# State-space convolution beside a feed-forward block on one core: borrowed PSUM banks and a new VectorE order at the outset, responses and another pair's first transform step in one run, the last token tile stored by halves

## The chip, the core and the metric

The kernel runs on one core of a Trainium2 chip, in one launch. The metric is the time of an execution in device microseconds. The engines are named as in the profile: PE is TensorE's matmul side and PEld its weight loads, DVE is VectorE, ACT is ScalarE, POOL is GpSimd, and SP is SyncE, which here only issues DMAs. PSUM has eight banks of 128 x 512 float32; a matmul writes into one of them, and ACT or DVE reads it out.

## The reference, cut to what matters

```python
xn = layernorm(u)                               # u: 2048 tokens x 576
h  = silu(xn @ w1)                              # w1: 576 x 4608
ffn = h @ w2                                    # w2: 4608 x 576
K[d, l] = Re(sum_n C[d,n] * dt[d]*B[d,n] * exp(dt[d]*A[d,n] * l))    # 128 states n, 2048 lags l
ssm = causal_convolution(xn, K) + xn * Dskip    # the reference does it by FFTs of length 4096
return u + ssm + ffn
```

All is float32 outside. Where the kernel multiplies in its faster float32 form it splits each operand into a high and a low part (names ending in `h` and `l`) and adds three products.

## The kernel before, in words

**Two streams.** A main stream, the generator `ffn`, does the feed-forward block. A side stream, the generator `side`, does everything else: loading and normalizing tokens, the convolution's kernel and spectra, and the stores. `weave` steps the main one and lets the side one go on at given marks. This gives the order of the program; a scheduler then plans the order of each engine's queue when the kernel is built, by a simulated timeline. `tc.high_priority()` moves instructions up in that plan, and `behind(ins)` forbids an instruction to stand ahead of `ins`. Each engine works through its queue in order, so an instruction that waits holds up all that is queued behind it.

**The feed-forward block.** 2048 tokens in two halves of two blocks of 512; 4608 hidden columns in nine chunks of four slots of 128. For a block and a chunk, `up` computes the slots (`ph`, L313 to L315: per slot 12 products of a 128-row part with `xh`/`xl` and two with the remaining 64 rows `x4`), ACT takes the SiLU out of PSUM (`gf`, L321) and casts it (`gh`, L322), DVE subtracts (`gl`, L323). `down` multiplies 128 tokens with the four slots, in two halves of 288 output columns (`po`, L338: 12 products each), and DVE adds the result to the token's sum (`acc`, L342). The weights of the next chunk come in meanwhile: `load_w1` and `load_w2` issue DMAs into `w1r` and `w2r` (L291), ACT casts them to `w1h` and `w2h` (L300), DVE subtracts to `w1l` (L282) and `w2l` (L302). At the turn from the first half of the tokens to the second, `next_xt` loads the transposed tokens `xl` (L352) on POOL's queue and `split_xt` splits them.

**PSUM banks.** `ps1` has two banks for `ph`, `ps2` three for `po`, and `pss` three for all of the side stream: token transposes `pt` (L124), `kp` and `z` (below), `pu` of the spread step, and the spectral step's products. A new tile of a pool waits until the oldest of its banks has been read out.

**The outset.** PE first runs filler matmuls on zeros (`idle`). `phase0` loads token tiles 0 to 7 by pairs into `acc`, on SP's queue alone or on SP's and ACT's; `norm` takes their statistics on DVE (L186), the inverse deviation `sd` on POOL, and normalizes; `put_xt` transposes on PE into `pt`, and ACT and DVE split that into `xh`, `xl`, `x4`. The later tiles 8 to 15 (`xj`) go through the same `norm` a little later, by `late`. The first chunk's slots are computed in two stretches of 256 columns, `up(blocks[0], t, 0, 256)` and then `(256, 512)`, because only the first tokens are there. `pins` holds the instructions behind which others are put: tiles 2 and 3 behind the first `w1l`, tiles 4 to 7 behind the last transposes' split of tile 3 (`xt3`), the four `w2l` behind the last `w1l`.

**Responses and transforms.** `kgen` computes the convolution's kernel for the 576 channels in 36 chunks of 16 channels. Per chunk DVE and ACT build tables `S` and `C` of sines and cosines times magnitudes (ACT: L631 and L633). Per two chunks (a pair; 18 in all) PE multiplies them into `kp` (L674, 64 products on 128x32 tiles into one bank), ACT copies it out (`kt`, L681), and PE applies the first step of a transform to `kt` (`z`, L689, eight products on 64x128 tiles into two banks); ACT copies `z` to `stage`, from which it is stored to DRAM every second pair. The kp products of a pair are held together by `behind(first)`, the z products likewise, so that each makes one run of PE's queue; po and ph of the main stream stand between the two. Each step of the side stream also takes the next step of `spread`, the tokens' own first transform: it copies and splits a tile (`sp`) and multiplies it in two halves, two products each (`pu`, L155, L156).

**The end.** The last `down` steps finish one token tile after the other; after them the tiles that are left are stored by `store`, in four quarters of 32 partitions on alternating queues (L177).

Of the kernel before, what the change touches and what calls it, by code (L numbers as in the profile page):

```python
# [11 lines left out]
F32 = mybir.dt.float32  # L12
# [3 lines left out]
ALU = mybir.AluOpType  # L16
# [3 lines left out]
P = 128  # L20
L = 2048
D = 576
NS = 128
FF = 4608
NJ = 16
NKT = 4
HD = D // 2
# [16 lines left out]
def kernel(  # L44
# [21 lines left out]
    nc = tc.nc  # L66
# [45 lines left out]
    acc = {}  # L112
# [23 lines left out]
    def behind(ins):  # L136
        return tc.issue_after(ins) if ins is not None else nullcontext()
# [36 lines left out]
    def store(t, j, engines):  # L174

        for ps, v, eng in quarters(ov, engines):
            eng.dma_start(v[:, j:j + 2] if len(t.shape) > 2 else v[:, j], t[ps])  # L177

    def norm(p0, js, xs):

        n = len(js)
        st = p0.tile([P, 2, 2, 6], F32, tag="st", name="st")
        mv = p0.tile([P, 2, 2], F32, tag="mv", name="mv")
        for i in range(n):
            for h in range(2):
                nc.vector.bn_stats(out=st[:, i, h, :], in_=xs[i][:, h * HD:(h + 1) * HD])  # L186
            nc.vector.bn_aggr(out=mv[:, i, :], in_=st[:, i, :, :])
        sd = p0.tile([P, 2], F32, tag="sd", name="sd")
        mb = p0.tile([P, 2], F32, tag="mb", name="mb")
        nc.vector.tensor_scalar(sd[:, :n], mv[:, :n, 1], 1e-5, None, op0=ALU.add)  # L190
        pins["sd"] = nc.gpsimd.tensor_tensor(sd[:, :n], sd[:, :n], mhalf[:, :n], op=ALU.pow).ins
        xn = p0.tile([P, 2, D], F32, tag="xn", name="xn") if js[0] < 8 else pairs[js[0]]
        for i, j in enumerate(js):
            if j % 2 == 0 or j < 2:
                pins["xn"] = nc.vector.tensor_scalar(xn[:, i, :], xs[i], mv[:, i, 0:1], sd[:, i:i + 1],
                                                 op0=ALU.subtract, op1=ALU.mult).ins
            else:
                nc.vector.scalar_tensor_tensor(mb[:, i:i + 1], mv[:, i, 0:1], -1.0, sd[:, i:i + 1],
                                               op0=ALU.mult, op1=ALU.mult)
                nc.scalar.activation(xn[:, i, :], xs[i], AF.Identity,  # L200
                                     scale=sd[:, i:i + 1], bias=mb[:, i:i + 1])
        return xn

    def phase0(p0, js, idle=None):

        xs = load_x(js[0], accp, "acc", (nc.sync, nc.scalar) if js[0] < 4 else (nc.sync,))
        acc.update(zip(js, xs))
        yield
        if js[0]:
            with behind(pins["w1l0"] if js[0] == 2 else None):  # L210
                normed(p0, js, xs)
        else:
            for j, xj in zip(js, xs):
                with behind(pins["xn"] if j else None):
                    normed(p0, (j,), (xj,))
                if not j:
                    pins["xt0s"] = pins["xt_s"]
                with behind(pins["pt"]):
                    idle(3 if j else 9)
        pins[f"xt{js[1]}h"] = pins["xt_h"]  # L220
        pins[f"xt{js[1]}"], pins[f"xt{js[1]}s"] = pins["xt_v"], pins["xt_s"]
        yield
# [23 lines left out]
    def ffn():  # L246
# [6 lines left out]
        def load_w1(half, c, t):  # L253

            f = c * FT + t
            first = half == 0 and c == 0
            last = half == 1 and c == NCH - 1
            r1 = (pa if first and t else yp if last and t else wp).tile([P, 5, 2 * P], F32, tag="w1r", name="w1r", bufs=1)
            fs = slice(f * P, (f + 2) * P)
            v1 = w1[0:512, fs].rearrange("(k p) f -> p k f", p=P)  # L260
            eng = nc.sync
            if first and t == 0:
                eng = nc.gpsimd
                nc.sync.dma_start(r1[:, 0:2, :], v1[:, 0:2])
                nc.scalar.dma_start(r1[:, 2:4, :], v1[:, 2:4])
            else:
                eng.dma_start(r1[:, 0:4, :], v1)
            eng.dma_start(r1[0:64, 4, :], w1[512:576, fs])
            pins["load"] = eng.dma_start(r1[64:128, 4, :], w1[512:576, fs]).ins
            R1[half, c, t] = r1  # L270

        def split_w1(half, c, t):
            first = half == 0 and c == 0
            r1 = R1.pop((half, c, t))
            for i in range(2):
                h1 = wp.tile([P, 5, P], F32R, tag="w1h", name="w1h", bufs=FT + 1)
                l1 = wp.tile([P, 5, P], F32R, tag="w1l", name="w1l", bufs=FT + 1)
                src = r1[:, :, i * P:(i + 1) * P]
                with behind(pins.get("gh", pins["xt1s" if t + i else "xt0s"])):
                    nc.scalar.copy(h1, src)  # L280
                with behind(pins["xn" if t else "xt1"] if first else None):
                    pins["w1l"] = nc.vector.tensor_sub(l1, src, h1).ins  # L282
                pins.setdefault("w1l0", pins["w1l"])
                W1[half, c, t + i] = h1, l1

        def load_w2(half, c, t):
# [7 lines left out]
        def split_w2(half, c, t):  # L294
            first = half == 0 and c == 0
            r2 = R2.pop((half, c, t))
            h2 = wp.tile([P, D], F32R, tag="w2h", name="w2h", bufs=FT + 1)
            l2 = wp.tile([P, D], F32R, tag="w2l", name="w2l", bufs=FT + 1)
            with behind(pins["xt_s"] if first else pins["gh"]):
                pins["w2h"] = nc.scalar.copy(h2, r2).ins  # L300
            with behind(pins["w1l"] if first else None):
                nc.vector.tensor_sub(l2, r2, h2)  # L302
            W2[half, c, t] = h2, l2

        def up(blk, t, a=0, e=512):
# [1 line left out]
            half, c, b = blk  # L307
            xh, xl, x4 = xts[2 * half + b]
            h1, l1 = W1[half, c, t]
            ph = ps1.tile([P, 512], F32, tag="ps1", name="ph")[:, a:e]  # L310
            for n, (w, v) in enumerate(((h1, xh), (h1, xl), (l1, xh))):
                for kt in range(NKT):
                    nc.tensor.matmul(ph, w[:, kt, :], v[:, kt, a:e], start=n + kt == 0, stop=False)  # L313
# [248 lines left out]
    def kgen():  # L562
        fT, phiT = kf["f"], kf["phi"]
        with tc.tile_pool(name="kg", bufs=1) as kg:
# [53 lines left out]
                return th  # L618

            stage = None  # L620
            tabs = []
            nxt = head(0)
            al = powers(0)
            for i in range(NCK):
# [52 lines left out]
                                if begins:  # L677
                                    first = mm.ins
                tabs = []
                kt = kg.tile([P, 512], F32, tag="kt", name="kt")  # L680
                nc.scalar.copy(kt, kp)  # L681

                z = [pss.tile([P, 512], F32, tag="pss", name="z") for _ in range(2)]
                first = None
                for eg in range(4):
                    for h in (1, 0):
                        rows = slice(64 * h, 64 * h + 64)
                        with tc.high_priority(), behind(first):
                            mm = nc.tensor.matmul(z[h][:, eg * P:(eg + 1) * P], kt[rows, eg * P:(eg + 1) * P], f1[rows],  # L689
                                                  start=True, stop=True, tile_position=(64 * h, 0))  # L690
                        first = first or mm.ins
                r = (i - 1) % NRUN
                if r == 0:
                    stage = kg.tile([P, 64, NRUN * CH], F32, tag="stage", name="stage")
                sv = stage[:, :, r * CH:(r + 2) * CH].rearrange("p k (e h c) -> p h e k c", h=2, c=2)
                for h in range(2):
                    nc.scalar.copy(sv[:, h], z[h].rearrange("p (e k c) -> p e k c", e=4, c=2))
                if r == NRUN - 2:
                    d0 = (i // NRUN) * NRUN * CH
                    kv = d1k.rearrange("(k n) (g d) -> g n k d", n=64, g=2)  # L700
                    for gp_ in range(2):
                        nc.sync.dma_start(kv[gp_, :, :, d0:d0 + NRUN * CH], stage[gp_ * 64:(gp_ + 1) * 64])
                yield (i + 1) / NCK

        nc.gpsimd.dma_start(d1k.rearrange("(k n) d -> n k d", n=P)[0],
# [135 lines left out]
    def side():  # L841
# [3 lines left out]
        with tc.tile_pool(name="kf", bufs=1) as kfp:  # L845
            for n in ("f", "phi"):
                kf[n] = kfp.tile([P, D], F32, name=n + "T")
            with tc.tile_pool(name="par", bufs=1) as par:
                with tc.tile_pool(name="pa", bufs=4) as pa:
# [17 lines left out]
                    next(p23)  # L867
                    yield 0
                    for js in ((4, 5), (6, 7)):
                        with behind(pins["xt3"]):  # L870
                            for _ in phase0(pa, js):
                                pass
                    kf["dt"] = steps()
# [127 lines left out]
```

## Time and profile before

| | |
|---|---|
| median of 3 runs | 1114.06 us (1113.56 to 1114.08) |
| profiled execution | 1113.42 us, its span 1111.6 us |
| granted TensorE clock | 1.0 |
| PE busy | 1103.3 us, 99% of the span, 9168 matmuls |
| DVE busy | 916.9 us, 82% |
| ACT busy | 709.2 us, 64% |
| POOL busy | 69.8 us, 6% |
| DMA | 148.56 MB, 134 GB/s on average |
| chain that ended last | PE 97%: po 42%, ph 41%, kp 3%, the spectral products 6%, z 2% |

The span is the time from the first to the last recorded event of the profiled execution; the execution's own time is 1.8 us longer. Rows of the trace show a start in microseconds from the span's beginning, a duration, engine and line, what the instruction writes and reads (`out<-in`, for a matmul with its tile of rows x columns), and the repeat count of equal neighbours; in brackets how long the engine stood before it and what ended the wait. The duration of a matmul includes its way through the array, so a step of PE is read from start to start.

### The profile page before, as it was taken

What the parts mean: (1) busy time and instruction counts of PE and PEld (TensorE: products, weight loads), DVE (VectorE), ACT (ScalarE), POOL (GpSimd) and SP (SyncE); (2) the same over time, 40 slices, a digit from 0 to 9 for tenths busy, and PEclk for the clock granted to TensorE, in tenths of its full rate; (3) what the DMA queues carried; (4) which work ended last, traced back from release to release, by engine and by line L of the source; (5) the groups of instructions that cost most, each with busy time, mean ns of one, the idle gap of its engine ahead of it and who ended that gap; (6) DMA issues with size and microseconds to landing.
All of it is one profiled execution on the core that took longest, in us unless ns stands there. A gap on an engine that the chain in (4) does not pass through costs nothing.

```text
span 1111.6 us, 22913 instructions
## 1 busy us (share of the span) xinstructions
PE 1103.3 (99%) x9168; PEld 997.8 (90%) x9168; DVE 916.9 (82%) x1546; ACT 709.2 (64%) x1228; POOL 69.8 (6%) x129
## 2 busy tenths in 40 slices
PE   8999999999999999999999999999999999999998
PEld 6998999899889899899989989999999999999887
DVE  6899899999999999999999837787778778784433
ACT  5574456676777676677866536877777878773210
POOL 1100000000000000011000000000000000000111
PEclk9999999999999999999999999999999999999999
DMA  9745522425242515255844163554545445434983
GB/s 258 201 122 152 137 71 61 120 63 130 82 107 80 134 61 131 77 149 161 219 123 105 44 173 106 169 157 128 161 145 150 139 146 171 129 107 130 248 211 86
DMA packets 175563, 148.56 MB, mean 134 GB/s; under 512 B 111024, under 2 KB 142272, under 8 KB 175328
## 3 DMA queue, kind: packets, MB, share of 16 engines
q1 hardware_dynamic: 165136, 112.33, 38.7%
q0 software_dynamic: 9568, 33.62, 9.5%
q8 instruction: 72, 1.18, 0.5%
q10 hardware_dynamic: 752, 1.15, 0.4%
q14 instruction: 35, 0.29, 0.1%
HBM read 102.53 MB, written 44.61 MB: 132 GB/s over the span
## 4 chain that ended last, share of the span: by engine, by line
PE 97%; DMA 1%; DVE 0%; SPq 0%; issue 0%; ACT 0%; ACTq 0%; POOL 0%; DVEq 0%
PE po L338 42%; PE ph L313 35%; PE kp L674 3%; PE ph L314 3%; PE ph L315 3%; PE pu L804 2%; PE pb L804 2%; PE pk L804 2%; PE z L689 2%; PE pu L155 1%; DMA acc<-in_A_u_dram 1%; PE py L825 1%; PE pu L156 1%; DMA w2r<-in_B_w_dram 0%; PE pt L124 0%; DVE st L186 0%
## 5 line engine op out<-in xcount | busy, mean ns | idle before, releaser
L338 PE MATMUL po<-w2l,gh 128*128 128x288 f32 x1152 | 338.5, 295 | 0.9 <-DVE w2l L302 0.9
L338 PE MATMUL po<-w2h,gl 128*128 128x288 f32 x1152 | 336.2, 295 | 0.0
L338 PE MATMUL po<-w2h,gh 128*128 128x288 f32 x1152 | 335.8, 295 | 0.0
L338 PEld LDWEIGHTS po<-w2h,gh 128*128 128x128 f32 x1152 | 215.1, 188 | 7.6 <-issue 2.8
L338 PEld LDWEIGHTS po<-w2l,gh 128*128 128x128 f32 x1152 | 215.9, 188 | 6.1 <-DVE w2l L302 1.1
L338 PEld LDWEIGHTS po<-w2h,gl 128*128 128x128 f32 x1152 | 215.4, 188 | 0.8
L321 ACT ACTIVATE gf<-ph 128x512 f32<-128x512 f32 (+1 forms) x148 | 86.4, 585 | 142.9 <-PE ph L315 128.3
L313 PE MATMUL ph<-xh,w1h 128*128 128x512 f32 (+1 forms) x592 | 162.1, 388 | 1.2 <-ACT gf L321 1.2
L313 PE MATMUL ph<-xl,w1h 128*128 128x512 f32 (+1 forms) x592 | 161.4, 386 | 0.0
L313 PE MATMUL ph<-xh,w1l 128*128 128x512 f32 (+1 forms) x592 | 161.0, 385 | 0.0
L342 DVE TENSOR_TENSOR acc<-po,acc 128x288 f32<-128x288 f32 x288 | 126.4, 452 | 37.4 <-PE po L338 36.1
L323 DVE TENSOR_TENSOR gl<-gf,gh 128x512 fp32r<-128x512 f32 (+1 forms) x148 | 99.2, 673 | 64.8 <-ACT gh L322 64.1
L313 PEld LDWEIGHTS ph<-xh,w1l 128*128 128x128 f32 x592 | 108.1, 188 | 19.9
L313 PEld LDWEIGHTS ph<-xl,w1h 128*128 128x128 f32 x592 | 108.0, 188 | 20.0 <-DVE xl L126 0.2
L313 PEld LDWEIGHTS ph<-xh,w1h 128*128 128x128 f32 x592 | 104.5, 188 | 18.5 <-ACT gf L321 1.8
L322 ACT CAST gh<-gf 128x512 fp32r<-128x512 f32 (+1 forms) x148 | 89.8, 609 | 10.1 <-PE po L338 7.1
L631 ACT ACTIVATE c<-th,magic 128x1040 f32<-128x1040 f32 x36 | 42.1, 1169 | 37.9 <-DVE C L654 28.0
L633 ACT ACTIVATE c<-th 128x1040 f32<-128x1040 f32 x36 | 38.7, 1075 | 34.0 <-DVE th L632 34.0
L300 ACT CAST w2h<-w2r 128x576 fp32r<-128x576 f32 x72 | 46.9, 671 | 17.2 <-PE po L338 14.9
L282 DVE TENSOR_TENSOR w1l<-w1r,w1h 128x640 fp32r<-128x640 f32 x72 | 57.1, 818 | 0.2
L314 PE MATMUL ph<-x,w1h 128*128 128x512 f32 (+1 forms) x148 | 57.0, 385 | 0.0
L315 PE MATMUL ph<-x,w1l 128*128 128x512 f32 (+1 forms) x148 | 56.9, 385 | 0.0
(184 smaller groups left out, 1830.1 us busy)
## 6 DMA issues: line engine op xcount, KB each, us to landing
w2r<-in_B_w_dram SPq DMA_DIRECT2D x72, 288.0 KB, 3.7
w1r<-in_B_w_dram SPq DMA_DIRECT2D x35, 512.0 KB, 3.9
d1u<-u POOLq DMA_DIRECT2D x32, 288.0 KB, 2.6
d1k<-stage SPq DMA_DIRECT2D x18, 512.0 KB, 6.8
ur<-d1u SPq DMA_DIRECT2D x32, 288.0 KB, 3.9
kr<-d1k SPq DMA_DIRECT2D x32, 288.0 KB, 2.8
d<-yo POOLq DMA_DIRECT2D x32, 288.0 KB, 3.7
ys<-d SPq DMA_DIRECT2D x32, 288.0 KB, 11.6
```

The lines of the kernel that those rows point to most:

```text
L282: pins["w1l"] = nc.vector.tensor_sub(l1, src, h1).ins
L300: pins["w2h"] = nc.scalar.copy(h2, r2).ins
L313: nc.tensor.matmul(ph, w[:, kt, :], v[:, kt, a:e], start=n + kt == 0, stop=False)
L314: nc.tensor.matmul(ph, h1[:, 4, :], x4[:, a:e], start=False, stop=False)
L315: pins["pe"] = nc.tensor.matmul(ph, l1[:, 4, :], x4[:, a:e], start=False, stop=True).ins
L321: nc.scalar.activation(gf, ph, AF.Silu)
L322: pins["gh"] = nc.scalar.copy(gh, gf).ins
L323: pins["gl"] = nc.vector.tensor_sub(gl, gf, gh).ins
L338: pins["pe"] = nc.tensor.matmul(po[:, :HD], G[blk, t][g][:, js], W2[half, c, t][w][:, hs], start=n == 0, stop=n == 3 * FT - 1).ins
L342: nc.vector.tensor_add(acc[j][:, hs], po[:, :HD], acc[j][:, hs])
L631: nc.scalar.activation(c65, th, AF.Identity, bias=magic)
L804: nc.tensor.matmul(dst, st, mv[:, hs], start=n == 0, stop=n == 3 * len(terms) - 1)
```

## The change

Three parts, with one hunk or more for each.

1. *The outset.* In the first stretch of 256 columns, slots 2 and 3 take their bank from `ps2` instead of `ps1`. The first `w1` load leaves POOL's queue: its last two pieces go on SP's and ACT's. Tiles 2 and 3 are loaded on SP's queue alone. The second pair of slots' `w1l` is allowed ahead of the normalization (behind `sdv`, the last DVE step ahead of POOL's part of the statistics) for its first slot; tiles 2 and 3 are put behind the last `w1l` instead of the first, and tiles 6 and 7 behind the last `w2l` instead of tile 3's transposes. One filler matmul of nine goes.
2. *Responses and transforms.* The z part of a pair is a function `along(first)`. It is called when the next pair's kp products have been issued, with the last of them as `first`, so that PE does `kp` of one pair and `z` of the pair before in one run. `kt` gets two buffers and waits in the list `kts`. The last pair's z comes behind its own kp copy.
3. *The last token tile.* `store` of tile 15 (`NJ - 1`) is done in two halves of 288 columns, four quarters each: eight DMAs of half the bytes.

```diff
     def store(t, j, engines):
-        for ps, v, eng in quarters(ov, engines):
-            eng.dma_start(v[:, j:j + 2] if len(t.shape) > 2 else v[:, j], t[ps])
+        for hs in (slice(0, HD), slice(HD, D)) if j == NJ - 1 else (slice(0, D),):
+            for ps, v, eng in quarters(ov, engines):
+                eng.dma_start(v[:, j:j + 2] if len(t.shape) > 2 else v[:, j, hs], t[ps] if len(t.shape) > 2 else t[ps, hs])
...
-        nc.vector.tensor_scalar(sd[:, :n], mv[:, :n, 1], 1e-5, None, op0=ALU.add)
+        pins["sdv"] = nc.vector.tensor_scalar(sd[:, :n], mv[:, :n, 1], 1e-5, None, op0=ALU.add).ins
...
     def phase0(p0, js, idle=None):
-        xs = load_x(js[0], accp, "acc", (nc.sync, nc.scalar) if js[0] < 4 else (nc.sync,))
+        xs = load_x(js[0], accp, "acc", (nc.sync, nc.scalar) if js[0] < 2 else (nc.sync,))
...
-            with behind(pins["w1l0"] if js[0] == 2 else None):
+            with behind(pins["w1l"] if js[0] == 2 else None):
                 normed(p0, js, xs)
...
-                    idle(3 if j else 9)
+                    idle(3 if j else 8)
...
             if first and t == 0:
-                eng = nc.gpsimd
+                eng = nc.scalar
                 nc.sync.dma_start(r1[:, 0:2, :], v1[:, 0:2])
-                nc.scalar.dma_start(r1[:, 2:4, :], v1[:, 2:4])
+                eng.dma_start(r1[:, 2:4, :], v1[:, 2:4])
             else:
-                eng.dma_start(r1[:, 0:4, :], v1)
-            eng.dma_start(r1[0:64, 4, :], w1[512:576, fs])
+                nc.sync.dma_start(r1[:, 0:4, :], v1)
+            nc.sync.dma_start(r1[0:64, 4, :], w1[512:576, fs])
             pins["load"] = eng.dma_start(r1[64:128, 4, :], w1[512:576, fs]).ins
...
-                with behind(pins["xn" if t else "xt1"] if first else None):
+                with behind(pins[("xn" if i else "sdv") if t else "xt1"] if first else None):
                     pins["w1l"] = nc.vector.tensor_sub(l1, src, h1).ins
-                pins.setdefault("w1l0", pins["w1l"])
...
             with behind(pins["w1l"] if first else None):
-                nc.vector.tensor_sub(l2, r2, h2)
+                pins["w2l"] = nc.vector.tensor_sub(l2, r2, h2).ins
...
         def up(blk, t, a=0, e=512):
-            ph = ps1.tile([P, 512], F32, tag="ps1", name="ph")[:, a:e]
+            pool, tag = (ps2, "ps2") if e == 256 and t > 1 else (ps1, "ps1")
+            ph = pool.tile([P, 512], F32, tag=tag, name="ph")[:, a:e]
...
             stage = None
+            kts = []
+
+            def along(first):
+                nonlocal stage
+                i, kt = kts.pop(0)
+                z = [pss.tile([P, 512], F32, tag="pss", name="z") for _ in range(2)]
+                for eg in range(4):
+                    for h in (1, 0):
+                        rows = slice(64 * h, 64 * h + 64)
+                        with tc.high_priority(), behind(first):
+                            mm = nc.tensor.matmul(z[h][:, eg * P:(eg + 1) * P], kt[rows, eg * P:(eg + 1) * P], f1[rows],
+                                                  start=True, stop=True, tile_position=(64 * h, 0))
+                        first = first or mm.ins
+                # (then z to stage, and stage to DRAM every second pair, as before)
...
                 tabs = []
-                kt = kg.tile([P, 512], F32, tag="kt", name="kt")
+                if kts:
+                    along(mm.ins)
+                kt = kg.tile([P, 512], F32, tag="kt", name="kt", bufs=2)
                 nc.scalar.copy(kt, kp)
-                # (the z part stood here, with first = None, and the copies to stage)
+                kts.append((i, kt))
+                if i + 1 == NCK:
+                    along(None)
                 yield (i + 1) / NCK
...
                     for js in ((4, 5), (6, 7)):
-                        with behind(pins["xt3"]):
+                        with behind(pins["xt3" if js[0] == 4 else "w2l"]):
                             for _ in phase0(pa, js):
                                 pass
```

More of the change, by code (lines that the diff above doesn't have):

```diff
@@ L620, in kgen @@
             stage = None
+            kts = []
[10 more added lines that the diff above has]
+                        first = first or mm.ins
+                r = (i - 1) % NRUN
+                if r == 0:
+                    stage = kg.tile([P, 64, NRUN * CH], F32, tag="stage", name="stage")
+                sv = stage[:, :, r * CH:(r + 2) * CH].rearrange("p k (e h c) -> p h e k c", h=2, c=2)
+                for h in range(2):
+                    nc.scalar.copy(sv[:, h], z[h].rearrange("p (e k c) -> p e k c", e=4, c=2))
+                if r == NRUN - 2:
+                    d0 = (i // NRUN) * NRUN * CH
+                    kv = d1k.rearrange("(k n) (g d) -> g n k d", n=64, g=2)
+                    for gp_ in range(2):
+                        nc.sync.dma_start(kv[gp_, :, :, d0:d0 + NRUN * CH], stage[gp_ * 64:(gp_ + 1) * 64])
             tabs = []
@@ L679, in kgen @@
                 tabs = []
-                kt = kg.tile([P, 512], F32, tag="kt", name="kt")
+                if kts:
+                    along(mm.ins)
+                kt = kg.tile([P, 512], F32, tag="kt", name="kt", bufs=2)
                 nc.scalar.copy(kt, kp)
[L683 to L702, printed above, removed]
+                kts.append((i, kt))
+                if i + 1 == NCK:
+                    along(None)
                 yield (i + 1) / NCK
```

## The prediction

> **What bounds the kernel now.** I read the page first (busy shares, then the chain that ended last), then the waits of TensorE, then the timeline of the first 35 us, of one pair of response chunks and of the end.
>
> ```profile
> span 1111.6 us, 22913 instructions
> ...
> PE 1103.3 (99%) x9168; PEld 997.8 (90%) x9168; DVE 916.9 (82%) x1546; ACT 709.2 (64%) x1228; POOL 69.8 (6%) x129
> ...
> PE ph L313 <- ACT gf L321: 1.2, 3, 0.5
> PE po L338 <- DVE w2l L302: 0.9, 1, 0.9
> ```
>
> PE is busy for 99% of the span and never waits longer than a microsecond for anybody. So only four things can move the time: where PE starts its real work, what it waits for, what its own switches between shapes cost, and what follows its last matmul. DVE at 82% and ACT at 64% matter where PE comes to wait for them. The profiled execution took 1113.42 us, 1.8 us more than its span and 0.64 us less than the median of the runs; I sum against the profiled one and add the result to the median, 1114.06. A measurement of this kernel can tell about 0.2%, 2.2 us, from no change.
>
> I worked the change out by laying the built order of each engine against the durations of the trace's rows: each instruction starts when its engine is free and what it waits for has ended. Laid on the old order this gives the old bank waits (0.69 us where the trace has 0.63), the wait for w2l, and no wait of PE between 45 us and the end, as in the trace; so I trust it where it gives waits for the new order. Where a landing decides I take the old landing.
>
> **The outset: what goes.**
>
> ```profile
> 6.81 0.82 DVE L186 BATCH_NORM_STATS2 st<-acc 128x6 f32<-128x288 f32 x2 [0.33 <-DMA acc<-in_A_u_dram]
> ...
> 10.72 0.74 PE L313 MATMUL ph<-xh,w1h 128*128 128x256 f32 x4
> ...
> 13.46 0.28 PE L314 MATMUL ph<-x,w1h 128*128 128x256 f32 x1
> ...
> 13.58 0.28 PE L315 MATMUL ph<-x,w1l 128*128 128x256 f32 x1
> ...
> 14.33 0.74 PE L313 MATMUL ph<-xh,w1h 128*128 128x256 f32 x4 [0.47 <-ACT gf L321]
> ...
> 24.70 0.74 PE L313 MATMUL ph<-xh,w1h 128*128 128x256 f32 x4 [0.24 <-ACT gf L321]
> ...
> 25.24 1.54 DVE L186 BATCH_NORM_STATS2 st<-acc 128x6 f32<-128x288 f32 x4 [2.00 <-DMA acc<-in_A_u_dram]
> ...
> 26.35 0.28 PE L315 MATMUL ph<-x,w1l 128*128 128x256 f32 x1
> ...
> 27.49 0.40 PE L338 MATMUL po<-w2l,gh 128*128 128x288 f32 x1 [0.86 <-DVE w2l L302]
> ```
>
> A step of 128x256 takes 0.12 us (13.46 to 13.58); from 13.58 to 14.33 it is 0.75, so a wait shown as 0.47 is 0.63 in starts. The page's 1.2 for three is this one, its twin and the 0.24 at 24.70; the three waits for a ps1 bank are then 0.63, 0.63 and 0.40, and each is followed by one step that is 0.10 longer: 1.97. Two borrowed ps2 banks remove all three. The wait for w2l is 27.49 - 26.35 - 0.12 = 1.02, and 0.10 behind it. It ends late because DVE stood 2.00 us at statistics whose tokens had not landed; the new order puts the four w2l ahead of those, so 1.12 goes. The two last pieces of the first w1 load leave POOL for SP and ACT, behind the first tokens, so DVE's 0.33 before 6.81 mostly goes: 0.25, and the eight instead of nine filler matmuls leave that room. Together 3.3 us.
>
> **The outset: what comes.** The new DVE order runs the statistics of tokens 8 and 9 (xj) ahead of two gl and of the first acc additions, while the old one ran them behind.
>
> ```profile
> 30.87 0.42 DVE L323 TENSOR_TENSOR gl<-gf,gh 128x256 fp32r<-128x256 f32 x1 [0.32 <-ACT gh L322]
> 31.21 1.53 DVE L186 BATCH_NORM_STATS2 st<-xj 128x6 f32<-128x288 f32 x4
> ...
> 33.64 0.60 PE L124 MATMUL pt<-ident,xn 128*128 128x128 f32 x4
> ```
>
> The fourth group of po needs the ps2 bank that the first acc addition frees. That addition now stands behind xj's statistics. Their tokens landed shortly before 31.21; SP has the same bytes queued ahead of them, so I take 30.4. Then 1.53 of statistics, 0.42 for gl, 0.46 for the addition (the row of the last one stands below) and some 0.1 of small steps: the bank is free at about 32.9. The matmul work ahead of that po is 19.3 us; with the small waits below PE would be there at 31.7. It waits 1.2 (0 if the tokens land 1.2 earlier, 2 if later by 0.8). For scale: the old order had done the same amount of work at 33.64.
>
> Four smaller waits come. The cast xh of tile 3 stood behind one gf on ACT; now gh and another gf stand ahead of it: 0.2, and 0.6 for the transposes of tile 3, whose pt banks wait for DVE. The splits of w1 for slots 2 and 3 now follow statistics of tiles 2 and 3: 0.15; w2l still ends 0.25 after PE wants it. The last transposes (tile 7) wait 0.9 for a pt bank. With 1.2 that is 3.3, and 0.10 behind each of six: 3.9. **Outset: 3.9 - 3.3, less 0.2 for overlap with small waits that the old order also had: +0.4 us** (from -1.5, no wait at po, to +1.2).
>
> **Responses and transforms in one run: what goes.**
>
> ```profile
> 169.88 0.29 PE L338 MATMUL po<-w2h,gh 128*128 128x288 f32 x1
> 170.01 0.29 PE L338 MATMUL po<-w2l,gh 128*128 128x288 f32 x1
> 170.23 0.28 PE L674 MATMUL kp<-C 128*32 128x64 f32 x4
> ...
> 171.98 0.31 PE L674 MATMUL kp<-S 128*32 128x64 f32 x6
> 172.22 0.54 PE L338 MATMUL po<-w2h,gl 128*128 128x288 f32 x2
> 172.60 0.29 PE L338 MATMUL po<-w2h,gh 128*128 128x288 f32 x1
> ...
> 177.15 0.39 PE L315 MATMUL ph<-x,w1l 128*128 128x512 f32 x1
> 177.37 0.39 PE L313 MATMUL ph<-xh,w1h 128*128 128x512 f32 x1
> 177.69 1.16 PE L689 MATMUL z<-f,kt 64*128 64x128 f32 x16
> 178.78 0.40 PE L155 MATMUL pu<-sp,s 128*128 128x288 f32 x1
> 179.02 0.30 PE L156 MATMUL pu<-sp,s 128*128 128x288 f32 x1
> ```
>
> This is what borders cost. Into kp: 170.01 to 170.23, 0.22 against 0.13 for a step of 128x288 (169.88 to 170.01): +0.09. Out of kp: the last six kp start from 171.98 on, some 0.02 apart, and po follows the last of them by 0.15, +0.14; the two po at 172.22 take 0.38 until 172.60 where 0.26 is usual, +0.11. Into z: 0.32 against 0.22 (177.15 to 177.37), +0.09. Out of z: the second pu starts 0.24 behind the first, +0.11. In the built order z of the pair before stands directly behind kp for 17 of 18 pairs. That removes one way out of kp (0.14 + 0.11) and one way into z (0.09), 0.34 a pair, and adds a border kp to z that the old trace does not have. Its ends are nothing (a step inside kp) and a way out and a way in together, 0.14 + 0.09. I take the 0.14 of kp's way out, the row that also ends a run of 128x32 tiles: 0.20 a pair, 3.4 us for 17 (1.9 to 5.8). The last pair has no kp to join and the built order cuts its z in two runs: one more border pair, +0.4. **Borders: -3.0.**
>
> The Trainium skill has a rule for this ("TensorEngine Tiling (Array Packing)", Key Properties): changing the tiling mode, not just the tile, drains TensorE. kp is 128x32 and z 64x128, so by it the border is not the cheap one and the gain is nearer 3.4 than 5.8. All the borders above agree with it; kp to z itself no run here shows.
>
> **What the run gives back.** Three pss banks serve kp, z, z and then pu of the spread step. kp's bank is freed by the copy kt on ACT, and the first pu takes it next. In the old order nothing wanted kt before z, 5.3 to 10.4 us behind the first kp. In the new one the first pu stands 4.3 to 6.7 us behind it (kp 1.84, z 0.89, borders, and 9 to 24 po between). With the rows of one pair:
>
> ```profile
> L681 ACT COPY kt<-kp x18: 561/572/588, 172.5 to 640.5; 128x512 f32<-128x512 f32 x18
> ...
> 382.27 0.34 PE L674 MATMUL kp<-C 128*32 128x64 f32 x8
> ...
> 385.54 1.17 ACT L631 ACTIVATE c<-th,magic 128x1040 f32<-128x1040 f32 x1 [3.31 <-DVE th L617]
> 386.61 0.56 ACT L681 COPY kt<-kp 128x512 f32<-128x512 f32 x1
> 389.77 1.07 ACT L633 ACTIVATE c<-th 128x1040 f32<-128x1040 f32 x1 [2.59 <-DVE th L632]
> ```
>
> kt ended 4.9 us behind kp here; over the 18 pairs it was 2.7 to 6.7. With the old lags against the new places three pairs would wait, 0.4, 0.7 and 0.3: 1.4. But kt also moves on ACT. In this pair it stood ahead of the cosine's L633; the built order now has gh, two w1h casts and L633 ahead of it, and L633 waits for DVE. That ends kt some 6.5 behind kp where pu stands at 5.2: 1.3 (0 with the old lag, 3 if L633 comes as late as here). Smaller waits of this kind at five other places add 1.2.
>
> The dearest place is where the next tokens come back.
>
> ```profile
> L291 SPq DMA_DIRECT2D w2r<-in_B_w_dram x1: 334/334/334, 494.6 to 494.6; - x1
> ...
> DMA to landing us min/median/max: 2.8/2.8/2.8
> ...
> L352 POOL DMA_DIRECT2D xl<-dxt x1: 773/773/773, 494.9 to 494.9; - x1
> ...
> L291 SPq DMA_DIRECT2D w2r<-in_B_w_dram x1: 328/328/328, 496.8 to 496.8; - x1
> ...
> DMA to landing us min/median/max: 8.1/8.1/8.1
> ```
>
> A w2r load issued behind POOL's xl load takes 8.1 us. The old order had the w2r that ACT casts first out at 494.6, ahead of xl, and it landed in 2.8. In the new order its buffer is freed by a w2l that comes later on DVE, so SP issues it after xl; w2h then holds up ACT with gh, two xh casts and L633, and kt behind them. PE waits 1.15 for w2h and 1.3 for kt (0 if the load gets out ahead, 5 if it lands as late as here). With 0.10 behind each of eight waits: 1.3 + 1.2 + 2.45 + 0.8, **5.75 back** (1.7 to 9).
>
> **The last tile by halves.**
>
> ```profile
> 1107.04 0.46 DVE L342 TENSOR_TENSOR acc<-po,acc 128x288 f32<-128x288 f32 x1 [1.14 <-PE po L338]
> 1107.52 0.78 SPq L177 DMA_DIRECT2D out_dram<-acc  x2
> ...
> DMA to landing us min/median/max: 1.6/1.9/2.0
> ```
>
> The last four stores are issued as before, behind the same addition, with half the bytes; the four of the first half go out during the 1.6 us of the second half's matmuls. Issue stays; of 1.6 to 2.0 us to landing I take 0.2 off (0 to 0.5). **Sum: +0.4 - 3.0 + 5.75 - 0.2 = +2.95 us:** 1116.4 for a profiled execution, 1117.0 against the median.
>
> **Rivals.** *Waits at the old lags* (chance 0.17). kt keeps the lags of the old trace and the w2r load gets out in time: waits of 1.4 and 0.3 behind them. 0.4 - 3.0 + 1.7 - 0.2 = -1.1: 1113.0. For it: ACT is busy only 64%. Against: kt's place on ACT has changed in the built order.
>
> *The banks come free in time* (0.18), the case on the other side. One mechanism: ACT reaches kt before pu is due, so that the borders' gain stands. It decides from 2.8 us of waits in the responses downwards (no slower than before), and from 0.6 downwards it is faster by what can be measured. 0.4 - 3.0 - 0.2 = -2.8, 1111.3; with kp to z as cheap as a step of kp -5.2, 1108.9. For it: PE waited nowhere in this stage. Against: the slack before was 0.8 to 4.6 us a pair, and the first pu has moved up by more than that at several pairs.
>
> *The loads share the engines* (0.07). If xl and w2r went side by side, w2r would land some 3 us after its issue and the 2.45 and 0.2 go: +0.3, 1114.4. The 8.1 us against 2.8 speak against it. The Trainium skill states such a rule ("DMA: Bandwidth & Descriptors", Queues, rings and completion order): each DMA engine takes turns between queue rows packet by packet. The trace's two landings 0.3 us apart do not look like turns.
>
> *ACT falls behind for good* (0.10). Each of the pairs whose kt now stands behind L633 waits like the one above: six more times 0.6, +6.55, 1120.6.
>
> *The change does not do what it says*: the last pair does not (costed), the other 17 do in the built order; no chance of its own.
>
> **How the numbers follow.** The forecast has 0.48, with its own range 1115.3 to 1119.1 (+1.2 to +5); about four fifths of it lie above 1116.3. With the last case that is slower 0.48. Faster: the free banks 0.18 and a tail of the old lags, 0.21. Within 0.2%: 0.31. Leaving out most of the 1120.6 case and the lower part of the free banks' case, the range is 1110.0 to 1119.8.
>
> **What would show it.** Right: TensorE's waits list pu L155 behind ACT kt near 390 and 505 us and po behind DVE acc near 32.9; no wait for gf before 30; z rows directly behind kp rows with a border near 0.15; span about 1114.4. Wrong: kt ending within 5 us of kp at every pair, or PE's waits after 45 us summing to under 3 us, makes the kernel no slower; a border of 0.3 would make it slower still.

## The result, and the profile after

The changed kernel took 1118.78 us in the median of six runs (1118.11 to 1120.94), the kernel before 1113.87 in six runs beside it: a ratio of 1.005, 95% interval 1.004 to 1.0061. It is slower by 4.9 us, where 1117.0 was forecast. The profiled execution took 1120.94 us, the longest of the six, so what is summed from its trace comes out 2.2 us above the median.

The page, then the waits of TensorE (engine, line, waited for; us in total, times, longest):

```profile
span 1119.2 us, 22932 instructions
...
PE 1103.2 (99%) x9167; PEld 999.2 (89%) x9167; DVE 917.1 (82%) x1546; ACT 706.5 (63%) x1228; POOL 70.1 (6%) x127
...
PE 78%; DVE 12%; DMA 4%; ACT 3%; issue 2%; SPq 0%; POOL 0%; DVEq 0%; ACTq 0%
```

```profile
PE pu L155 <- ACT kt L711: 3.3, 4, 1.1
PE po L339 <- DVE acc L343: 1.8, 1, 1.8
PE pt L124 <- DVE xn L196: 1.3, 2, 1.1
...
PE ph L314 <- ACT gf L322: 1.1, 1, 1.1
PE pt L128 <- DVE xl L126: 1.0, 2, 0.7
PE po L339 <- DVE w2l L302: 0.8, 2, 0.6
...
PE po L339 <- ACT w2h L300: 0.3, 1, 0.3
```

PE's busy time is the same to 0.1 us. Before, the chain that ended last was 97% PE; now DVE has 12%, DMA 4% and ACT 3% of it, because it is handed over at each wait of PE to whoever ended that wait and follows that engine back for a while. The list says where: four waits for kt (none before), one for an acc addition (none before), and one of 1.1 for gf that is not an outset wait, as its place shows below.

Where in time the loss came: the first kp of the changed kernel and its last two steps.

```profile
172.63 0.34 PE L702 MATMUL kp<-C 128*32 128x64 f32 x8
...
1115.06 0.46 DVE L343 TENSOR_TENSOR acc<-po,acc 128x288 f32<-128x288 f32 x1 [1.14 <-PE po L339]
```

Before, these stood at 170.23 and 1107.04. So this execution lost 2.4 us up to the first kp, 5.6 from there to the last addition, and won 0.4 behind it (1119.2 - 1115.06 against 1111.6 - 1107.04): +7.6, the difference of the spans.

The joined runs and the last pair:

```profile
200.79 0.31 PE L702 MATMUL kp<-S 128*32 128x64 f32 x6
201.03 1.16 PE L634 MATMUL z<-f,kt 64*128 64x128 f32 x16
202.12 0.40 PE L339 MATMUL po<-w2l,gh 128*128 128x288 f32 x1
...
652.45 0.30 PE L339 MATMUL po<-w2h,gl 128*128 128x288 f32 x1
652.67 1.16 PE L634 MATMUL z<-f,kt 64*128 64x128 f32 x8
653.76 0.40 PE L339 MATMUL po<-w2h,gh 128*128 128x288 f32 x1
...
654.75 1.16 PE L634 MATMUL z<-f,kt 64*128 64x128 f32 x8
```

z follows the last kp by 0.15 us (the six kp start some 0.02 apart from 200.79), at all 17 joined pairs. Read the last pair by its counts: a whole z run is x16 in 1.16 us, each half of the cut one is x8 and takes 1.16 as well. A cut z costs twice, not once with two more borders.

One of the four waits for kt, on ACT and on PE:

```profile
391.19 1.16 ACT L659 ACTIVATE c<-th,magic 128x1040 f32<-128x1040 f32 x1 [1.92 <-DVE th L618]
392.26 0.61 ACT L323 CAST gh<-gf 128x512 fp32r<-128x512 f32 x1
392.76 1.35 ACT L281 CAST w1h<-w1r 128x640 fp32r<-128x640 f32 x2
394.02 1.07 ACT L661 ACTIVATE c<-th 128x1040 f32<-128x1040 f32 x1
394.99 0.56 ACT L711 COPY kt<-kp 128x512 f32<-128x512 f32 x1
...
395.61 0.40 PE L155 MATMUL pu<-sp,s 128*128 128x288 f32 x1 [1.12 <-ACT kt L711]
```

ACT stood behind DVE until 391.19 and then had a step of the cosine, gh, two w1h casts and the cosine's next step ahead of kt, as the built order said. And the wait of 1.1 for gf at the end of the stage, on SP, ACT and PE:

```profile
625.27 3.59 SPq L647 DMA_DIRECT2D d1k<-stage  x2
629.29 8.95 SPq L291 DMA_DIRECT2D w2r<-in_B_w_dram  x3
...
636.42 0.68 ACT L300 CAST w2h<-w2r 128x576 fp32r<-128x576 f32 x1 [2.88 <-DMA w2r<-in_B_w_dram]
...
643.16 1.21 PE L314 MATMUL ph<-xh,w1h 128*128 128x512 f32 x4 [1.11 <-ACT gf L322]
```

The stage store has moved by a pair with its z and now leaves just ahead of the w2r loads. The first w2r lands 7.1 us after its issue (636.4), ACT waits 2.88 for it, and the gf that PE needs comes late. Before, no store left between 600 and 645 us, and the four w2r loads of that stretch landed like this:

```profile
L291 SPq DMA_DIRECT2D w2r<-in_B_w_dram x4: 328/334/583, 604.6 to 623.0; - x4
...
DMA to landing us min/median/max: 2.9/3.0/4.5
```

### The profile page after: what moved, and what is told of

The parts are those of the page before. It is cut to its first block, busy times and chain, and to the rows that moved or that the text cites. A ratio compares the mean times of both kernels' runs of the same rounds, so it can differ in the third digit from the quotient of the medians.

```text
span 1119.2 us, 22932 instructions
## 1 busy us (share of the span) xinstructions
PE 1103.2 (99%) x9167; PEld 999.2 (89%) x9167; DVE 917.1 (82%) x1546; ACT 706.5 (63%) x1228; POOL 70.1 (6%) x127
## 4 chain that ended last, share of the span: by engine, by line
PE 78%; DVE 12%; DMA 4%; ACT 3%; issue 2%; SPq 0%; POOL 0%; DVEq 0%; ACTq 0%
PE po L339 33%; PE ph L314 28%; PE ph L315 2%; PE ph L316 2%; PE pu L816 2%; PE pb L816 2%; PE pk L816 2%; PE kp L702 2%; DMA w2r<-in_B_w_dram 1%; DVE th L616 1%; DVE C L670 1%; DVE acc L343 1%; PE z L634 1%; DVE S L681 1%; DVE gl L324 1%
## 5 line engine op out<-in xcount | busy, mean ns | idle before, releaser
L659 ACT ACTIVATE c<-th,magic 128x1040 f32<-128x1040 f32 x36 | 42.0, 1166 | 46.1 <-DVE C L682 30.8
L302 DVE TENSOR_TENSOR w2l<-w2r,w2h 128x576 fp32r<-128x576 f32 x72 | 53.6, 751 | 4.4 <-ACT w2h L300 4.3
```

Source lines behind the costliest of these rows:

```text
L302: pins["w2l"] = nc.vector.tensor_sub(l2, r2, h2).ins
L659: nc.scalar.activation(c65, th, AF.Identity, bias=magic)
```

## The experiments

Three kernels take one part of the change each; the rest is the kernel before.

**The outset alone.**

> Only the first part of the change (borrowed banks, order at the outset) on the kernel before. Theory (tiles 8 and 9's statistics stand on DVE ahead of the first acc additions, and the fourth po waits for a bank): no wait for gf but one, a wait of about 1.9 of po behind DVE acc near 33, a wait of 0.7 of pt near 45; outset +1.5 to +2, time 1115.2 to 1116. Rival (the borrowed banks' 3.1 us come through and the loss lies in the responses): 1110.8 to 1112.

1113.46 us, 1.0002 of the kernel before (0.9994 to 1.0011): no change, neither theory's time. TensorE's waits between 10 and 50 us, of this kernel:

```profile
PE pt L128 <- DVE xl L126: 1.0, 2, 0.7
PE ph L313 <- DVE w1l L282: 0.2, 1, 0.2
...
PE ph L313 <- ACT xh L125: 0.2, 1, 0.2
```

The waits for gf and w2l (2.1 in sum) are gone, 1.6 came (the row left out has 0.2). The wait of po for the acc addition is not there in this execution: xj's tokens let DVE start at 30.30, in the profile of the whole change only at 32.62:

```profile
32.62 1.54 DVE L187 BATCH_NORM_STATS2 st<-xj 128x6 f32<-128x288 f32 x4 [3.03 <-DMA xj<-in_A_u_dram]
...
35.19 0.40 PE L339 MATMUL po<-w2h,gh 128*128 128x288 f32 x1 [1.84 <-DVE acc L343]
```

With the same order of the first 45 us, three profiles have 0, 0.9 and 1.8 us for that wait. It hangs on the landing.

**The joined runs alone.**

> Only the second part (kp of one pair and z of the pair before in one run) on the kernel before. Theory (borders gain 3.0, waits for kt, w2h and gl give back 5.5 to 6.5): pu waits for kt at four places, 3.3 us in sum, span +2.5 to +3.5, time 1116.5 to 1117.5. Rival (the borders' gain stands and the outset cost the time): 1111. The wait of 1.3 at the end of the stage (near 641 in the changed kernel), which the forecast did not have: if it belongs to this part, it is here too and the time is 1117.5 to 1119.

1119.19 us, 1.006 (1.0046 to 1.0075): +5.7, the whole loss and a little more, and just above the 1117.5 to 1119 expected with the wait near 640.

```profile
PE pu L155 <- ACT kt L710: 3.4, 4, 1.2
PE ph L313 <- ACT gf L321: 2.0, 4, 0.8
...
PE po L338 <- ACT w2h L300: 1.3, 1, 1.3
```

The same four waits for kt are here, and a fourth wait for gf of 0.8 near 640 beside the three of the outset: it belongs to this part. The w2h wait came near 446. It is not proper to the joined order: the kernel with the third part alone (below), whose order there is the old one, waited 1.0 for w2h at the same place, and the kernel before not at all. The rival, 1111, is out.

**The halves alone.**

> Only the third part (the last tile stored by halves) on the kernel before. Theory: 0.2 to 0.4 less from the last matmul to the end of the span, 1113.6. Rival (the half stores' own issue and fixed landing time make up for the bytes): 0.0, 1113.9.

1113.3 us, 0.9999 (0.999 to 1.0007). In its trace the end comes 4.25 us after the start of the last addition (1108.85 to 1113.1), 4.56 before: 0.3 less, as the theory has it, and too little for the times to tell it from nothing.

**kt ahead of the cosine.** The waits for kt could be a sign of something slower behind them, so ACT's order alone was changed:

```diff
-                nc.scalar.activation(c65, th, AF.Abs)
+                with behind(pins.get("kt")):
+                    nc.scalar.activation(c65, th, AF.Abs)
...
-                nc.scalar.copy(kt, kp)
+                pins["kt"] = nc.scalar.copy(kt, kp).ins
```

> The second part alone, and on ACT the cosine's absolute value of the next chunk is put behind kt, so that kt no longer stands behind an instruction that waits for DVE. Theory (kt's place on ACT is what costs): no wait of pu for kt in the trace, some 2.4 us of waits near 231 to 237 stay, time 1113.8 to 1114.8, 2.5 to 3.5 less than the second part alone. Rival (late w2r loads behind the stage stores, or DVE, set the pace, and kt is only what shows): the waits move to po and ph, and the time stays at that of the second part alone within 0.7.

No pu waited for kt, and the waits near 235 came as expected, but the median was 1118.51 (1.0042 of the kernel before, 1.0029 to 1.0054), in runs of 1116.3 to 1117.2 and of 1119.8 to 1120.6. The profiled run, 1120.59, had a wait of 1.0 for w2h near 389, and one that neither theory named: the first py (the products that end the convolution) stood 2.2 us near 1040 for ys, which is loaded from DRAM, and the granted clock behind it was 0.50 from 1042 to 1044. Its new order has the last spectral product closer to the first py (18 instead of 22 us), so that its store and the loads behind it come late. The pin had also moved the w2r loads near 620 ahead of the stage store (issued at 618.9 and 620.5, the store at 627.1), where the joined runs alone have them behind it. So the time says little for either theory; the pin had moved other parts.

**The stage store on another queue.**

```diff
-                        nc.sync.dma_start(kv[gp_, :, :, d0:d0 + NRUN * CH], stage[gp_ * 64:(gp_ + 1) * 64])
+                        nc.gpsimd.dma_start(kv[gp_, :, :, d0:d0 + NRUN * CH], stage[gp_ * 64:(gp_ + 1) * 64])
```

> The second part alone, with the stores of stage issued on POOL's queue instead of SP's. Theory (the eighth pair of stage stores, moved by a pair to just ahead of the w2r loads on SP's queue, makes w2r land some 7 us after its issue, w2h late on ACT, and PE wait 1.0 to 1.3 for gf near 640): w2r issued near 625 to 632 lands in 3 to 4 us, the wait near 640 is gone, time 1.0 to 1.5 below the second part alone, 1117.7 to 1118.3. Rival (that landing was chance, or the stores' bytes and not their place on SP's queue slow w2r): the wait stays, the time stays within 0.4 of 1119.2.

1125.67 us, 1.0109 (1.0093 to 1.0124): 11.4 above the kernel before, where the joined runs alone have 5.7 and less was expected. The DMA issues between 629 and 638 us (KB each, median us to landing):

```profile
d1k<-stage POOLq DMA_DIRECT2D x2, 512.0 KB, 9.0
w2r<-in_B_w_dram SPq DMA_DIRECT2D x2, 288.0 KB, 6.5
d1u<-u POOLq DMA_DIRECT2D x1, 288.0 KB, 9.2
```

w2r had SP's queue to itself and still took 6.5 us. So the place on SP's queue is not needed for the delay, and that theory falls. The rival's mechanism, that the store's bytes slow the load, stands; in a version below, where the w2r loads leave ahead of the store, the first is there 3.0 us after its issue (617.30, cast at 620.27). The rival's time does not stand, as it expected no change. The Trainium skill ("DMA: Bandwidth & Descriptors", Queues, rings and completion order) says that each DMA engine serves its queue rows in turn, packet by packet; this fits it. On POOL the store also held up the d1u store behind it, which frees u1 for the spread step, and the longest wait for kt grew from 1.2 to 2.1. The larger part of what was added is w2h: four waits, 4.7 in sum (1.8 near 574, 1.6 near 447, 0.9 near 640), against one of 1.3.

**The pin again, with the tail put right.** A mark of 0.595 instead of 0.597 at the end of the stage gives the last spectral product its old distance from the first py. First with the store on POOL and part three:

> The second and third parts, kt pinned on ACT as before, stage stores on POOL's queue, and the second mark 0.595 instead of 0.597, which puts the last spectral product as far ahead of the first py as in the kernel before. Theory: no wait of pu for kt, none near 640, none of py for ys; waits of 2.4 near 231 to 237 stay and the last pair's z is still cut (1.3): borders -3.4 + 1.3 + waits 2.4 + 0.5 - tail 0.2 = +0.6, time 1113.5 to 1115. Rival (joined runs leave something else behind that the waits don't show): 1116 or more, as the earlier pinned version's median.

1117.08 us, 1.0029 (1.0018 to 1.004), against 1114.31 beside it: +2.8, more than the theory's bound. No wait for kt, for ys or near 640; but some 2 us (from start to start) of small waits near 533 to 573 that were not foreseen. The number is the rival's, though what was left behind does show in the waits.

Then the whole change with the same three edits:

> The whole change with kt pinned on ACT, stage stores on POOL's queue and the second mark 0.595. Theory (the loss of the whole change lies in kt's place and the late w2r loads; the outset is neutral): 1113.5 to 1115.5, some 4 below the changed kernel. Rival (the outset's po wait adds its 2 us when the responses are mended): 1116 to 1117.5.

1117.82 us, 1.0034 (1.0021 to 1.0047): +3.5, 0.7 above the one without the outset, with 0.9 of po waiting for acc and one wait for kt, 0.5 near 479, that the pin did not remove. Some 1.4 less than the changed kernel's loss of 4.9, a third of what was expected.

Then without the outset, with the store back on SP, where the queues' traffic changes and the orders of TensorE and VectorE do not:

> The joined and pinned version with mark 0.595 and halves, its stage stores back on SP's queue (TensorE's and VectorE's orders are the same as in the version with the stores on POOL). Theory (the stores' bytes slow a w2r load on whichever queue they go, and on POOL's they also hold up the d1u stores): 0 to 1 below the POOL version, 1.001 to 1.003 of the kernel before. Rival (the place on SP's queue holds w2r up): 0.5 to 1.3 above it.

1114.92 us, 1.0016 (1.0007 to 1.0025) against 1113.37: +1.5. It was 2.8 with the store on POOL; the intervals overlap, but the rival's sign is not there. The pair does not test a store just ahead of the w2r loads, however: in both versions the loads leave first (here at 617.30, the store at 625.62). Its waits, and who waited for kt:

```profile
PE po L339 <- DVE gl L324: 1.6, 1, 1.6
PE ph L314 <- ACT gf L322: 1.3, 4, 0.5
...
PE po L339 <- ACT w2h L301: 1.0, 1, 1.0
PE pu L155 <- DVE sp L151: 0.4, 1, 0.4
```

```profile
L712 ACT COPY kt<-kp x18: 563/582/590, 171.2 to 642.3; 128x512 f32<-128x512 f32 x18
...
who waited for it (us, times):
busy tenths in 40 slices 0000000000000000000000000000000000000000
```

Nobody waited for kt. From the joined runs alone to this kernel the loss went from 5.7 to 1.5 us. This is the test of the main reason: some 4 us went when ACT took kt in time. The waits for kt, 3.4 and 0.1 behind each, are the larger part. But they are not all of it: the wait near 640 went because the w2r loads now leave ahead of the stage store, and the mark and the halves (0.3) stand in the same comparison.

**The same without the join.**

> The same pin of ACT, mark 0.595 and halves, without the joined runs: z behind its own pair's kt as in the kernel before. Theory (with kt in time the join itself is worth 17 x 0.20 less 1.3 for the last pair's cut, -2.1): with as many waits it is 2 above the joined one; the waits of 2.4 near 235 belong to the joined order and are not here, so that the time is 0 to 0.6 below the joined one, within 0.2% of the kernel before at 1114. Rival (the pin itself, not the join, brings the waits near 235 and the loss that is left): 2 above the joined one, 1.004 of the kernel before.

1114.55 us, 1.0009 (1.0 to 1.0018): 0.4 below the joined one, within the forecast's 0 to 0.6 though the intervals overlap. The 1.6 near 235 is not there, so it belongs to the joined order. With kt in time the join neither wins nor loses anything that can be measured: what the borders save (2.1) is paid near 235, at gl (1.6) and sp (0.4). Pin, mark and halves are in both kernels of this pair, so it asks about the join alone, as far as the plan, which differs too, lets it; the joined runs alone and the kernel before do the same. The join cost 5.7 us where kt came late and 0.4 where it came in time.

**z by halves.** The cut of the last pair raised a question about the array, asked of the kernel before by swapping two loops:

```diff
-                for eg in range(4):
-                    for h in (1, 0):
+                for h in (1, 0):
+                    for eg in range(4):
```

> The kernel before with the loops of z swapped: the four products of one bank, then the four of the other, in one run as before, where they alternated. Theory (products of the two 64-row halves run side by side, so that a cut along the banks doubles a z run): a run of z takes 1.77 instead of 0.88 us, 18 x 0.89 = +16, with some 1 of waits for w2h: 1129 to 1131.5. Rival (the forecast's: only the borders of a run count): 1113.5 to 1115.

```profile
177.48 1.26 PE L689 MATMUL z<-f,kt 64*128 64x128 f32 x16
178.68 0.40 PE L155 MATMUL pu<-sp,s 128*128 128x288 f32 x1
```

A run by halves takes 1.26 us, 0.1 more than the alternating one, not 0.9. The +16 did not come; 18 x 0.1 did. The two halves run side by side also when one is queued behind the other, as long as they stand in one run. What doubles the cost is other work between them, as in the cut pair. The Trainium skill ("TensorEngine Tiling (Array Packing)", Key Properties) says that different tiles can work in parallel; the 1.26 shows it across four queued products. The time, 1121.39 (1.0063, 1.0044 to 1.0081), is neither theory's; it holds other waits: 2.6 for w2h near 443 and 1.9 of py for ys.

**xj's statistics later, at the outset.** The calls for tiles 8 and 9 at marks 0.022 and 0.024 instead of 0.004 and 0.005, on the outset alone:

> The first part alone, with the statistics of tiles 8 and 9 called later in the program, behind the first acc additions. Theory (the outset gains its 3 us and gives them back to xj's statistics on DVE): no wait of po for acc near 33 and none of pt near 45, TensorE's 45 us mark 0.9 to 2 us of work further than in the first part alone; the plan behind it changes too, with waits of 0.3 to 1.4 near 450, 505 and 536, so the time is 1113 to 1115. Rival (the outset has nothing to gain): the first 45 us as in the first part alone.

Waits between 10 and 50 us:

```profile
PE ph L313 <- ACT w1h L280: 0.4, 1, 0.4
PE pt L128 <- DVE xl L126: 0.3, 1, 0.3
...
```

No wait for acc and 0.7 less of pt, as expected: 1.1 in sum, with 0.2 each for two rows left out, against 2.1 before the change. Counted in usual steps, TensorE had begun 32.4 us of matmul work by the 45 us mark, against 30.8 in the first part alone, as the theory has it. That this is a gain of the outset is not shown: traces with the old outset have 30.2 to 32.2 by then. And the time was 1120.04, 1.0064 (1.0049 to 1.0079), against 1113 to 1115 expected: the plan behind it changed at many places, with 1.6 of po waiting for gl near 539 and 1.9 of py for ys. No version here beats the kernel before.

## Why the prediction was right, and which steps were off

*The sign and the case.* The forecast was that the joined runs give back more than the borders save, at about 1117.0; measured 1118.78, inside the range and the forecast's own 1115.3 to 1119.1. The part that was forecast to lose did (+5.7 alone), the others did not move the time. That the waits of the responses come out as near as they do is in part luck: of 1.15 that was counted near 505 only 0.25 came, and 1.3 that was not counted came near 642 (both below).

*What bounds it.* PE did wait longer than a microsecond before: 1.28 us at the very start, for the zeros of the filler matmuls. All traces have it, so no difference rests on it.

*Outset, +0.4.* Measured 0.0 alone. The waits that were to go went, and those that came are the ones named, at their places. The 1.2 for xj was right as a middle: 0 to 1.8 by the landing. In the profiled execution of the whole change it fell at 1.8, and with pt and w1h beside it made 2.4; that is this execution's share, not the change's. The 1.12 that was to go with w2l is a landing's work too: of the nine traces with the old outset four have that wait (0.6 to 1.3 us) and five have none, as the tokens that DVE's statistics need land earlier (DVE stood 0.54 us there in the joined runs alone, 2.00 before). So the sum took as gain what a run of the old kernel may not lose.

*Borders, 0.20 a pair.* kp to z measured 0.15, the 0.14 that was taken from kp's way out. 17 x 0.20 = 3.4 stands. The rule that the prediction took from the Trainium skill ("TensorEngine Tiling (Array Packing)", Key Properties), that a change of the tiling mode drains TensorE, agrees with the 0.15, against 0.02 for a step inside kp. *The last pair's cut, 0.4*, was mis-sized: it counted one more border pair, but each half of z also takes as long as a whole (1.16 us). The two halves with their borders (0.22 into one and 1.09 to the next start, 0.11 behind, less the 0.13 of a usual step) took 2 x 1.29 where one run takes 1.29: 1.3 more, so the borders' sum is -2.1 and not -3.0.

*kt, the main mechanism.* Near 390 the lag of 6.5 us behind kp and the wait of 1.3 came as worked out (in starts 394.20 to 395.61, that is from the start of one step to the start of the next, less a usual step), the one near 505 with 1.3 too. Only the wait for DVE stood a step earlier than in the working: near 390 ahead of L659, the old L631, and not at the old L633. Near 340 and 369 it was 0.8 and 0.6 in starts, where the "smaller waits" at five places were to make 1.2. The four together are 3.9, against 3.8 in the forecast.

*w2h near 505, 1.15.* Measured 0.25 in starts (506.58 to 506.96; the cast w2h ended at 506.91). The w2r behind xl landed in 4.6 us, not 8.1. The 0.3 for w2h in the list of waits is another one, near 448, where nothing was forecast.

*What the sum left out.* The step failed at "where a landing decides I take the old landing". z took its stage store along by a pair; that store was costed at nothing. It put w2r's landing at 7.1 us, and PE waited 1.3 in starts near 642 (1.0 in the joined runs alone). Together the waits behind the first kp make some 7.5 in this profile where 5.75 stood (in starts 3.9 for kt, 1.3 near 642, 0.7 for w2h and w2l near 448 and 451, 0.7 in three short ones near 235, 237 and 507 that the list does not show, and 0.1 behind most of them); less the 2.1 of the borders that is 5.4, against the 5.6 read between the two rows above.

*Halves, -0.2.* 0.3 to 0.4 in the traces, not measurable in the times.

*The rivals.* "The banks come free in time" asked for less than 0.6 of waits; 3.3 were there for kt alone. Mended so that kt is in time, the joined runs still did not win, which that rival would have had. "ACT falls behind for good" is out: four pairs waited, not all that had kt behind the cosine. "The loads share the engines" was turned down on the 8.1 us; the store on POOL shows that loads do share, only not in a way that makes w2r quick. Near 505 half of it came true: the w2r landed in 4.6 us and most of the wait for w2h did not come, but the one for kt did.

*Open.* Of the 1.5 that is left in the pinned joined version 1.2 is there without the join too, with intervals that overlap; how much of it is the pin, the mark or the plan isn't separated; a pin of one instruction changes the plan hundreds of microseconds away, so that orders which differ by it also differ elsewhere. A version that keeps the last z whole was not run.

## What to carry to other kernels

Joining two short stages saves borders that can be read from the trace to 0.01 us, but it also moves up whoever takes the freed bank next: set the lag of the copy that frees it against the new place of its next user, at every pair, before counting the gain. Count what travels with a moved step, its DMAs above all, and look which loads they now meet. And when a scheduler plans the order, an experiment's edit changes the plan far from it: read the window of the trace that the edit is about, and trust the total only where the other orders are the same.

## What the runs showed of the hardware that was not expected

Products on the two 64-row halves overlap even when one half's four are queued behind the other's four (1.26 us against 1.16), and one half alone takes as long as both (1.16).

After some long waits the array is slow. The kernel with z by halves, around its wait for w2h (us, busy and count of each engine, granted clock, DMA share, GB/s):

```profile
442.60:445.60 3.00, 0.38 (x3) 0.14 (x2) 3.00 (x7) 0.72 (x2) 0.00 (x0) 0.97 0.62 202
445.60:449.60 4.00, 3.99 (x19) 3.98 (x19) 4.00 (x6) 2.56 (x3) 0.00 (x0) 0.60 0.30 77
449.60:453.60 4.00, 4.00 (x34) 3.51 (x33) 2.21 (x4) 2.65 (x4) 0.00 (x0) 1.00 0.09 23
```

For 4 us after it the granted clock is 0.60, some 1.6 us lost on top of the wait. The 1.9 of py near 1040 in the same kernel was followed by 0.50 over 3 us, a wait of 2.1 in the kernel with its store on POOL by 1.00, and one of 1.9 in the version with xj's statistics later by 1.00 too, so a wait of this size costs more only at times. The Trainium skill ("TensorE: Matmul & The Clock Gate", Part 1) gives about 3.4 us for the idle window after which the clock is halved; here shorter waits did it. In the changed kernel the clock was 1.00 behind its waits.
